# Slots chosen by transposes, unit 0 in two column parts, and an earlier third chunk of w_out

## The chip, the core and the metric

The kernel runs on one core of one Trainium2 chip. The time is the device time of one execution in microseconds (us), and the median of three runs is the measure. The chain of engines is TensorE (PE; PEld is its weight loading), VectorE (DVE), ScalarE (ACT), GpSimd (POOL), which has nothing to do here, and SyncE (SP), whose queue issues the transfers.

## What is computed

Three layers in a row. Sigmoid attention (4 batches, 12 heads, 448 tokens, 64 wide) gives x of 1792 tokens by 768. A soft mixture of 8 experts with 4 slots each (32 slots) follows, and then a last layer with a cosine gate:

```python
slot_input = d.T @ x                       # 32 slots x 768
h = np.maximum(slot_input[e] @ w1[e], 0.0) # per expert, 4 slots
slot_out[e] = h @ w2[e]
x = c @ slot_out                           # 1792 x 768
h = x @ w_in                               # 768 x 2048
g = h * np.cos(h)
out = g @ w_out                            # 2048 x 768
```

w_in and w_out come as 64-bit floats and are narrowed to 32 bits on the chip.

## The kernel before

The last layer never forms x. It first makes M = slot_out @ w_in, 32 slots by 2048 columns, and then h = c M per block. M is laid out in the tile m4 as four parts of 32 rows (twice the high part of M, twice its rest), and ct4 holds the weights c in the same four parts, so that one matmul of 128 by 128 by 448 gives h of one unit.

**The second expert layer.** The experts go in two groups g of four. w2_rows and part multiply a group's 16 wide slots (four column strips of 32) by w2 as it lands, into PSUM tiles e2[g, k] (k = 0: 512 columns, k = 1: 256). Only the diagonal blocks of these are wanted. w2_out copies e2 to SBUF (for group 1 the left half on ScalarE and the right half on VectorE). choose then makes, for each 128 columns of the model (chunk c, six of them), a product with the small 0/1 tile pick, which both turns the chunk and picks the 16 slots. twice copies the result from PSUM to s_acc with every slot doubled.

**M.** wide_m(so, c, pairs) adds chunk c's share to M's first 512 columns, in strips of 64 rows (the doubled slots): pair 0 and pair 1 are two PSUM tiles of 2 x 128 columns. rest_m does the same for the other 1536 columns, in four strips of 32 rows side by side. m_hi and m_lo write m4's parts for the first four f. m_split does it for the rest: one cast on ScalarE (mh), one difference on VectorE (ml), and 16 transfers that spread them to m4.

**Units.** A unit u = (t, f) is a block of 448 columns of tokens by 128 columns of w_in. wave(u) is its h matmul, in one of two PSUM banks (ps_h), and ScalarE's scaling; wave_end is ScalarE's rounding; frac(u) is VectorE's centring and ScalarE's sine; product(u) is VectorE's h * cos(h) and the last reader of the h bank, so the h matmul of unit u + 2 waits for product(u). out_unit(u, os) multiplies the result by the chunk f of w_out, six tiles o of 128 rows. For the first SOME = 6 units this is a full 32-bit product in two passes. From unit 6 on it is three products of rounded parts, which need wh and wl.

**w_out.** A chunk f is narrowed by wo_abs(f), one ScalarE step of 768 columns, and wo_steps(f), three VectorE steps. Then wo_hi(f) on ScalarE and wo_lo(f) on VectorE make the parts wh and wl, and wo_lo loads chunk f + 6 into the raw tile that is free.

**Order.** Every engine runs its instructions in the order in which the program gives them (manual_schedule). Up to unit 1 the order is written out by hand (lines 1012 to 1058). From then on a loop over u issues, for each unit: product(u + 1), upper, frac(u + 2), the first two output tiles of u, wave(u + 3), steps from the list later (some_of), lower, the other four tiles. The list holds wo_abs, wo_steps, wo_hi and wo_lo in order with a price each (0.55, 0.95, 0.95 for the steps, 0.95 for wo_lo, nothing for those of ScalarE). A unit brings a budget of 3.6 in the first six units and 1.9 later, and the list is worked off from its head while the budget lasts.

Of the kernel before, what the change touches and what calls it, by code (L numbers as in the profile page):

```python
# [10 lines left out]
F32 = mybir.dt.float32  # L11
# [14 lines left out]
P = 128  # L26
# [35 lines left out]
def fused(ctx: ExitStack, tc: tile.TileContext, qk, vv, phi, w1, w2, w_in, w_out, out):  # L62
# [629 lines left out]
    def wide_m(so, c, pairs=range(2)):  # L692

        for i in pairs:
            for n in range(2):
                at = (2 * i + n) * P
                nc.tensor.matmul(  # L697
                    m_ps[i][n * D:(n + 1) * D, 0:P], so.rearrange("p r s -> p (r s)"), wi[:, c, at:at + P],
                    start=c == 0, stop=c == KD - 1,
                )  # L700

    def rest_m(so, c):

        for j in range(4):
            at = MC + 3 * P * j
            nc.tensor.matmul(  # L706
                m_ps[2][j * NS:(j + 1) * NS, 0:3 * P], so[:, 0], wi[:, c, at:at + 3 * P],
# [4 lines left out]
    def so4_of(c):  # L712
        return s_acc.rearrange("p a f -> p (a f)")[:, c * 2 * NS:(c + 1) * 2 * NS].rearrange("p (r s) -> p r s", r=2)

    so2 = s_acc.rearrange("p a f -> p (a f)")[:, 512:512 + 4 * NS].rearrange("p (c r s) -> p c r s", c=2, r=2)

    with ExitStack() as ex:
# [3 lines left out]
        with tc.manual_schedule():  # L721
# [67 lines left out]
            def w2_out(g, k):  # L789

                n = 256 if k else 512
                if g == 0:
                    nc.scalar.copy(sos[g, k], e2[g, k][:, 0:n])
                    return
                nc.scalar.copy(sos[g, k][:, 0:n // 2], e2[g, k][:, 0:n // 2])
                nc.vector.tensor_copy(sos[g, k][:, n // 2:n], e2[g, k][:, n // 2:n])

            def choose(g, k):

                for c in range(2 if k else 4):  # L800
                    at = (256 if k else 0) + c * NS + 16 * g
                    nc.tensor.matmul(
                        (e2[0, 1] if k else ps_so)[:, at:at + 16], sos[g, k][:, c * P:(c + 1) * P],
                        pick[:, g], start=True, stop=True,
                    )

            def twice(out, chosen, n):

                nc.vector.tensor_copy(
                    out, chosen.rearrange("p (c s) -> p c s", c=n).unsqueeze(2).to_broadcast([P, n, 2, NS])  # L810
                )
# [11 lines left out]
            pick = exp_.tile([P, 2, NS // 2], F32, name="pick")  # L823
            for g in range(2):
                for j in range(4):
                    at = 36 * j + 16 * g
# [320 lines left out]
```

## Time and profile before

| | before |
|---|---|
| median of 3 runs | 528.34 us (528.27 to 529.23) |
| the profiled execution | 528.16 us, span of the core 526.5 us |
| PE busy | 507.0 us (96% of the span) |
| DVE busy | 302.7 us (57%) |
| ACT busy | 301.3 us (57%) |
| DMA | 98.91 MB, 188 GB/s on the mean |
| mean granted TensorE clock | 0.999 |

The attention and the first expert matmuls take the first 215 us. From 215 to 258 us TensorE waits for w2 as it lands. The stretch that the change edits lies between 239 and some 285 us. From there to the end TensorE runs the units. Times in the rows are us from the span's start. A busy PE is not PE at its peak, since matmuls are pipelined and their ends are modelled: the start of the next one tells how long one holds the engine. A full 32-bit matmul stands as two records (passes).

### The profile page before, as it was taken

The numbers are of one execution on the slowest core, as the hardware profiler recorded it, in microseconds if no ns is written. First come the engines' busy times: TensorE is split into PE (matmuls) and PEld (weight loads), VectorE is DVE, ScalarE is ACT, GpSimd is POOL, SyncE is SP. The second block draws the span as 40 slices with busy tenths as digits, with TensorE's granted clock in tenths as the row PEclk, the third lists the DMA queues.
The fourth block names the chain that finished last, engine by engine and source line by source line (L and its number), as shares of the span: only waits on it lengthen the run. The fifth ranks groups of instructions, "written<-read, shape, count | busy, mean of one in ns | idle before, by whom it ended". The sixth has DMA issues, their size and how long they took to land.

```text
span 526.5 us, 8037 instructions
## 1 busy us (share of the span) xinstructions
PE 507.0 (96%) x3134; PEld 321.9 (61%) x3134; DVE 302.7 (57%) x591; ACT 301.3 (57%) x488; POOL 2.1 (0%) x16
## 2 busy tenths in 40 slices
PE   8999999999999997968999999999999999999997
PEld 4333333334334532314544599999999999999996
DVE  4545895685683324300179897999664464564442
ACT  5877768668667310200158687887665555555551
POOL 1000000000000000000000000000000000000000
PEclk9999999999999999999999999999999999999999
DMA  6798899787447899999954331330020020020002
GB/s 227 240 338 309 296 332 359 255 333 270 151 150 247 264 407 415 414 415 413 390 210 110 120 120 61 120 121 2 0 106 0 2 105 1 9 98 0 1 0 105
DMA packets 30117, 98.91 MB, mean 188 GB/s; under 512 B 3200, under 2 KB 11264, under 8 KB 30080
## 3 DMA queue, kind: packets, MB, share of 16 engines
q1 hardware_dynamic: 30080, 98.42, 51.9%
q8 instruction: 24, 0.39, 0.3%
q14 instruction: 13, 0.11, 0.1%
HBM read 92.11 MB, written 5.51 MB: 185 GB/s over the span
## 4 chain that ended last, share of the span: by engine, by line
PE 83%; DMA 11%; DVE 3%; ACT 1%; issue 1%; SPq 0%
PE o L994 43%; PE av L315 14%; DMA w<-in_w 11%; PE sc L295 11%; PE h L945 3%; PE xn L335 2%; PE idle L371 1%; PE lg L362 1%; PE h L734 1%; PE so L773 1%; PE sl L502 1%; PE m L706 1%; DVE wi L1006 1%; PE lt L386 1%; PE m L697 1%
## 5 line engine op out<-in xcount | busy, mean ns | idle before, releaser
L994 PE MATMUL o<-gh,wl 128*128 128x448 f32 x348 | 126.4, 363 | 0.0
L994 PE MATMUL o<-gl,wh 128*128 128x448 f32 x348 | 126.3, 363 | 0.0
L994 PE MATMUL o<-gh,wh 128*128 128x448 f32 x348 | 125.9, 362 | 0.0
L304 ACT ACTIVATE a<-sc,bias_s 128x896 f32<-128x896 f32 x72 | 70.3, 1006 | 31.7 <-PE sc L295 31.6
L994 PEld LDWEIGHTS o<-gh,wl 128*128 128x128 f32 x348 | 65.5, 188 | 5.4 <-issue 0.2
L994 PEld LDWEIGHTS o<-gh,wh 128*128 128x128 f32 x348 | 65.2, 187 | 4.8 <-issue 0.2
L994 PEld LDWEIGHTS o<-gl,wh 128*128 128x128 f32 x348 | 65.3, 188 | 3.5
L315 PE MATMUL av<-a,v 128*64 128x448 f32 x288 | 64.7, 556 | 0.0
L974 ACT CAST gh<-wi 128x448 fp32r<-128x448 f32 x58 | 32.8, 566 | 51.5 <-PE o L994 44.5
L960 DVE SCALAR_TENSOR_TENSOR wi<-wi 128x448 f32<-128x448 f32 x63 | 39.2, 622 | 35.1 <-ACT wi L953 35.1
L979 DVE TENSOR_TENSOR gl<-wi,gh 128x448 fp32r<-128x448 f32 x58 | 36.2, 624 | 33.0 <-ACT gh L974 32.6
L947 ACT ACTIVATE wi<-h 128x448 f32<-128x448 f32 x63 | 34.1, 542 | 26.7 <-PE h L945 26.1
L295 PEld LDWEIGHTS <-hi 64*128 64x128 f16 x384 | 19.4, 95 | 37.6 <-issue 20.2
L968 DVE TENSOR_TENSOR wi<-h,wi 128x448 f32<-128x448 f32 x63 | 38.9, 617 | 0.9 <-ACT wi L963 0.9
L773 PE MATMUL so<-w,zone 128*32 128x256 f32 (+1 forms) x256 | 31.5, 490 | 7.8 <-DMA w<-in_w 7.8
L963 ACT ACTIVATE wi<-wi 128x448 f32<-128x448 f32 x63 | 36.2, 575 | 2.6 <-DVE wi L960 2.6
L953 ACT ACTIVATE wi<-wi 128x448 f32<-128x448 f32 x63 | 36.4, 578 | 2.0
L295 PE MATMUL sc<-hi 64*128 64x448 f16 x192 | 35.2, 359 | 0.4 <-ACT a L304 0.4
L315 PEld LDWEIGHTS av<-a,v 128*64 128x64 f32 x288 | 16.4, 135 | 29.9 <-issue 29.2
L295 PE MATMUL sc<-hi,lo 64*128 64x448 f16 x192 | 34.4, 354 | 0.3
L295 PE MATMUL sc<-lo,hi 64*128 64x448 f16 x192 | 34.3, 354 | 0.0
L273 DVE CAST hi<-raw 128x896 f16<-128x896 f32 x23 | 14.3, 624 | 34.3 <-DMA raw<-in_qk 34.2
(175 smaller groups left out, 573.2 us busy)
## 6 DMA issues: line engine op xcount, KB each, us to landing
w<-in_w SPq DMA_DIRECT2D x28, 768.0 KB, 15.1
w<-in_w SPq DMA_DIRECT2D x30, 512.0 KB, 6.4
wi<-in_w_in SPq DMA_DIRECT2D x24, 512.0 KB, 6.9
wo<-in_w_out SPq DMA_DIRECT2D x16, 768.0 KB, 4.5
w<-in_w SPq DMA_DIRECT2D x11, 1024.0 KB, 7.1
raw<-in_qk SPq DMA_DIRECT2D x23, 448.0 KB, 3.9
v<-in_vv SPq DMA_DIRECT2D x24, 224.0 KB, 4.3
out_t<-wi SPq DMA_DIRECT2D x24, 224.0 KB, 2.0
```

Source lines behind the costliest of these rows:

```text
L295: nc.tensor.matmul(ps[:, j, 0:S], keys[at, first:first + P], q[at, 0:S], start=n == 0, stop=n == len(terms) - 1)
L304: nc.scalar.activation(a[at], ps[at], AF.Sigmoid, bias=bias_s[at[0]], scale=qk_scale)
L315: nc.tensor.matmul(av[i][js, 0:S], v32[i][:, vc:vc + D], a[:, j], start=g == 0, stop=g == 3)
L773: nc.tensor.matmul(e2[g, k][j * NS:(j + 1) * NS, 0:n], h1[g][:, c, j * NS:(j + 1) * NS], w(j), start=c == 0, stop=c == F // P - 1,)
L947: nc.scalar.activation(ph, h, AF.Copy, bias=0.25, scale=inv2pi)
L953: nc.scalar.activation(tn, ph, AF.Copy, bias=magic)
L960: nc.vector.scalar_tensor_tensor(out=ph, in0=tn, scalar=-magic, in1=ph, op0=ALU.add, op1=ALU.subtract)
L963: nc.scalar.activation(tn, ph, AF.Sin, scale=-2.0 * math.pi)
L968: nc.vector.tensor_mul(g, hs.pop(u), tn)
L974: nc.scalar.copy(gs[u][1], gs[u][0])
L979: nc.vector.tensor_sub(gs[u][2], gs[u][0], gs[u][1].bitcast(F32))
L994: nc.tensor.matmul(ps, w[:, cols], g, start=begins and n == 0, stop=ends and n == len(terms) - 1)
```

## The change

The change edits five things.

- choose turns each chunk with a transpose instead of a product with pick, and a new keep_slots copies the wanted columns with one strided VectorE copy, once and not doubled. pick and twice are gone. w2_out of group 1 is one ScalarE copy. The slots of chunks 0 to 3 lie in l_all, of 4 and 5 in s_acc (slots_of).
- wide_m has four strips of 32 rows instead of two of 64.
- Unit 0's scaling, rounding, centring, sine, product and outputs are done in two halves of 224 columns (first, second).
- m_split is cut in two (m_split_hi, m_split_lo), and the hand-written order is a new one. In it chunk 2 of w_out is narrowed whole ahead of unit 2 (wo_abs(2) behind unit 1's sine, wo_steps(2, 3) behind unit 1's product), and wo_abs(3) stands ahead of wave(3). The list later no longer has these steps.
- wave(4) stands behind all of unit 1's outputs and behind what the list issues there. The warming matmuls of one of three steps are gone.

```diff
--- before.py
+++ after.py
@@ -692,11 +692,11 @@
     def wide_m(so, c, pairs=range(2)):
 
         for i in pairs:
-            for n in range(2):
-                at = (2 * i + n) * P
+            for k in range(4):
+                at = (2 * i + k // 2) * P
                 nc.tensor.matmul(
-                    m_ps[i][n * D:(n + 1) * D, 0:P], so.rearrange("p r s -> p (r s)"), wi[:, c, at:at + P],
-                    start=c == 0, stop=c == KD - 1,
+                    m_ps[i][k * NS:(k + 1) * NS, 0:P], so, wi[:, c, at:at + P], start=c == 0,
+                    stop=c == KD - 1,
                 )
 
     def rest_m(so, c):
@@ -704,15 +704,16 @@
         for j in range(4):
             at = MC + 3 * P * j
             nc.tensor.matmul(
-                m_ps[2][j * NS:(j + 1) * NS, 0:3 * P], so[:, 0], wi[:, c, at:at + 3 * P],
+                m_ps[2][j * NS:(j + 1) * NS, 0:3 * P], so, wi[:, c, at:at + 3 * P],
                 start=c == 0, stop=c == KD - 1,
             )
 
 
-    def so4_of(c):
-        return s_acc.rearrange("p a f -> p (a f)")[:, c * 2 * NS:(c + 1) * 2 * NS].rearrange("p (r s) -> p r s", r=2)
-
-    so2 = s_acc.rearrange("p a f -> p (a f)")[:, 512:512 + 4 * NS].rearrange("p (c r s) -> p c r s", c=2, r=2)
+    def slots_of(c):
+
+        if c < 4:
+            return l_all.rearrange("p b c s -> p (b c s)")[:, 256 + c * NS:256 + (c + 1) * NS]
+        return s_acc.rearrange("p a f -> p (a f)")[:, 512 + (c - 4) * NS:512 + (c - 3) * NS]
 
     with ExitStack() as ex:
         zone = ex.enter_context(reuse("zone", bufs=1)).tile([P, 2 * F], F32, name="zone")
...
-                n = 256 if k else 512
-                if g == 0:
-                    nc.scalar.copy(sos[g, k], e2[g, k][:, 0:n])
-                    return
-                nc.scalar.copy(sos[g, k][:, 0:n // 2], e2[g, k][:, 0:n // 2])
-                nc.vector.tensor_copy(sos[g, k][:, n // 2:n], e2[g, k][:, n // 2:n])
+                nc.scalar.copy(sos[g, k], e2[g, k][:, 0:256 if k else 512])
 
             def choose(g, k):
 
+                ps = (e2[0, 1][:, 256:] if k else ps_so).rearrange("p (c m) -> p c m", m=P)
                 for c in range(2 if k else 4):
-                    at = (256 if k else 0) + c * NS + 16 * g
-                    nc.tensor.matmul(
-                        (e2[0, 1] if k else ps_so)[:, at:at + 16], sos[g, k][:, c * P:(c + 1) * P],
-                        pick[:, g], start=True, stop=True,
-                    )
-
-            def twice(out, chosen, n):
-
+                    nc.tensor.transpose(ps[:, c], sos[g, k][:, c * P:(c + 1) * P], ident)
+                return ps
+
+            def keep_slots(g, k, ps):
+
+                out = (s_own[:, 512:512 + 2 * NS] if k else l_own[:, 256:]).rearrange("p (c s) -> p c s", s=NS)
+                v = ps[:, :, 16 * g:16 * g + 4]
                 nc.vector.tensor_copy(
-                    out, chosen.rearrange("p (c s) -> p c s", c=n).unsqueeze(2).to_broadcast([P, n, 2, NS])
+                    out[:, :, 16 * g:16 * g + 16].rearrange("p c (j k) -> p c j k", j=4),
+                    bass.AP(v.tensor, v.offset, [v.ap[0], v.ap[1], [36, 4], v.ap[2]]),
                 )
 
             def keep_warm(n):
...
-            pick = exp_.tile([P, 2, NS // 2], F32, name="pick")
-            for g in range(2):
-                for j in range(4):
-                    at = 36 * j + 16 * g
-                    nc.vector.tensor_copy(pick[:, g, 4 * j:4 * j + 4], ident[:, at:at + 4])
             w1_group(0)
             w1_group(1)
             nc.scalar.activation(sine, ident[:, 0:1], AF.Sin)
-            so4 = s_own[:, 0:8 * NS].rearrange("p (c r s) -> p c r s", c=4, r=2)
...
             for c in range(0, F // P - 2, 2):
                 w2_rows(1, c)
                 if c == 0:
-                    choose(0, 0)
-                    choose(0, 1)
-                keep_warm(4)
+                    ps = [choose(0, k) for k in range(2)]
+                    for k in range(2):
+                        keep_slots(0, k, ps[k])
+                if c < F // P - 4:
+                    keep_warm(4)
...
-            choose(1, 0)
+            ps = choose(1, 0)
             part(1, 1, F // P - 2, lambda j: w[:, 0, j], 256)
+            keep_slots(1, 0, ps)
+            m_ps.update({k: bank((4, 3, 5)[k], f"m{k}") for k in range(3)})
+            for c in range(2):
+                wide_m(slots_of(c), c, [0])
             part(1, 1, F // P - 1, lambda j: w[:, 1, j], 256)
-            twice(so4, ps_so[:, 0:4 * NS], 4)
             w2_out(1, 1)
-            m_ps.update({k: bank((4, 3, 5)[k], f"m{k}") for k in range(3)})
-            for c in range(4):
-                wide_m(so4[:, c], c, [0])
-            choose(1, 1)
-            twice(so2, e2[0, 1][:, 256:256 + 2 * NS], 2)
-            for c in range(2):
-                wide_m(so4[:, c], c, [1])
+            for c in range(2, 4):
+                wide_m(slots_of(c), c, [0])
+            keep_slots(1, 1, choose(1, 1))
+            wide_m(slots_of(0), 0, [1])
 
 
     wctx.close()
@@ -911,17 +904,25 @@
         src, hi, lo = m_parts(f)
         nc.vector.tensor_sub(lo, src, hi.bitcast(F32))
 
-    def m_split():
-
-        mh, ml = [ring[:, (12 + k) * S:(12 + k) * S + 3 * P] for k in range(2)]
-        nc.scalar.copy(mh.bitcast(F32R), m_ps[2][:, 0:3 * P])
-        nc.vector.tensor_sub(ml.bitcast(F32R), m_ps[2][:, 0:3 * P], mh)
-        for j in range(4):
+    mh, ml = [ring[:, (12 + k) * S:(12 + k) * S + 3 * P] for k in range(2)]
+
+    def spread(js, groups):
+
+        for j in js:
             cols = slice(MC + 3 * P * j, MC + 3 * P * (j + 1))
-            for g in range(4):
+            for g in groups:
                 nc.sync.dma_start(
                     out=m4[g * NS:(g + 1) * NS, cols].bitcast(F32), in_=(mh, ml)[g // 2][j * NS:(j + 1) * NS]
                 )
+
+    def m_split_hi():
+        nc.scalar.copy(mh.bitcast(F32R), m_ps[2][:, 0:3 * P])
+        spread([0], (0, 1))
+
+    def m_split_lo():
+        nc.vector.tensor_sub(ml.bitcast(F32R), m_ps[2][:, 0:3 * P], mh)
+        spread([0], (2, 3))
+        spread(range(1, 4), range(4))
 
     SOME = 6
     units = [(t, f) for t in range(2) for f in range(SOME)] + [(2, f) for f in range(NF)]
@@ -936,7 +937,28 @@
 
     hs, tmp = {}, {}
 
-    def wave(u, rounded=True):
+    first, second, whole_s = slice(0, S // 2), slice(S // 2, S), slice(0, S)
+
+    def scaled(u, cols):
+        nc.scalar.activation(tmp[u][0][:, cols], hs[u][:, cols], AF.Copy, bias=0.25, scale=inv2pi)
+
+    def rounded(u, cols):
+        nc.scalar.activation(tmp[u][1][:, cols], tmp[u][0][:, cols], AF.Copy, bias=magic)
+
+    def centred(u, cols):
+        ph, tn, g = tmp[u]
+        nc.vector.scalar_tensor_tensor(
+            out=ph[:, cols], in0=tn[:, cols], scalar=-magic, in1=ph[:, cols], op0=ALU.add, op1=ALU.subtract
+        )
+
+    def sined(u, cols):
+        nc.scalar.activation(tmp[u][1][:, cols], tmp[u][0][:, cols], AF.Sin, scale=-2.0 * math.pi)
+
+    def times(u, cols):
+        ph, tn, g = tmp[u]
+        nc.vector.tensor_mul(g[:, cols], hs[u][:, cols], tn[:, cols])
+
+    def wave(u, both=True):
         if u >= len(units):
             return
         t, f = units[u]
@@ -944,29 +966,20 @@
         h = hs[u] = ps[:, 0:S]
         nc.tensor.matmul(h, m4[:, f * P:(f + 1) * P], ct4[:, t * S:(t + 1) * S], start=True, stop=True)
         ph, tn, g = tmp[u] = [spare[k] if u == 0 else buf(3 * (u % 4) + k) for k in range(3)]
-        nc.scalar.activation(ph, h, AF.Copy, bias=0.25, scale=inv2pi)
-        if rounded:
-            wave_end(u)
-
-    def wave_end(u):
-        ph, tn, g = tmp[u]
-        nc.scalar.activation(tn, ph, AF.Copy, bias=magic)
+        scaled(u, whole_s if u else first)
+        if u and both:
+            rounded(u, whole_s)
 
     def frac(u):
 
-        if u >= len(units):
-            return
-        ph, tn, g = tmp[u]
-        nc.vector.scalar_tensor_tensor(
-            out=ph, in0=tn, scalar=-magic, in1=ph, op0=ALU.add, op1=ALU.subtract
-        )
-        nc.scalar.activation(tn, ph, AF.Sin, scale=-2.0 * math.pi)
+        if u < len(units):
+            centred(u, whole_s)
+            sined(u, whole_s)
 
     def product(u):
         if u < len(units):
-            ph, tn, g = tmp.pop(u)
-            nc.vector.tensor_mul(g, hs.pop(u), tn)
-            gs[u] = [g]
+            times(u, whole_s)
+            gs[u] = [tmp.pop(u)[2]]
 
     def upper(u):
         if SOME <= u < len(units):
...
+    def out_half(cols, os):
+
+        for o in os:
+            if cols == first:
+                acc[o] = bank(o, f"o0_{o}")
+            nc.tensor.matmul(
+                acc[o][:, cols], whole(0)[:, o * P:(o + 1) * P], gs[0][0][:, cols],
+                start=cols == first, stop=False,
+            )
 
     def out_unit(u, os):
         t, f = units[u]
@@ -1011,51 +1034,62 @@
     with tc.manual_schedule():
         for f in range(A_SLOTS, WO_SLOTS):
             load_wo(f)
-        both = [so4_of(c) for c in range(4)] + [so2[:, c] for c in range(2)]
+        both = [slots_of(c) for c in range(KD)]
         wo_abs(0, 2)
         wide_m(both[4], 4, [0])
         wide_m(both[5], 5, [0])
-        wo_steps(0)
         m_hi(0, nc.vector.tensor_copy)
         m_lo(0)
         m_hi(1)
+        wide_m(both[1], 1, [1])
         wide_m(both[2], 2, [1])
-        wide_m(both[3], 3, [1])
         wave(0)
+        wo_steps(0, 2)
+        m_lo(1)
+        for c in range(3, KD):
+            wide_m(both[c], c, [1])
+        rounded(0, first)
+        centred(0, first)
+        scaled(0, second)
+        sined(0, first)
+        rounded(0, second)
         wo_steps(0)
-        m_lo(1)
-        wo_steps(0, 2)
-        wide_m(both[4], 4, [1])
-        wide_m(both[5], 5, [1])
-        for c in range(2):
-            rest_m(both[c], c)
-        wave(1, False)
-        frac(0)
-        wave_end(1)
-        wo_steps(0)
-        for c in range(2, 4):
-            rest_m(both[c], c)
-        wo_abs(1)
-        product(0)
-        wo_steps(0)
+        times(0, first)
+        centred(0, second)
+        rest_m(both[0], 0)
+        rest_m(both[1], 1)
         m_hi(2)
         m_hi(3)
-        frac(1)
+        wave(1, False)
+        sined(0, second)
+        rounded(1, whole_s)
+        wo_abs(1)
+        wo_steps(0)
         m_lo(2)
         m_lo(3)
-        out_unit(0, range(3))
-        for c in range(4, KD):
+        times(0, second)
+        gs[0] = [tmp.pop(0)[2]]
+        out_half(first, range(3))
+        rest_m(both[2], 2)
+        out_half(second, range(3))
+        wo_steps(0, 2)
+        frac(1)
+        wo_abs(2)
+        for c in range(3, KD):
             rest_m(both[c], c)
+        m_split_hi()
+        wo_steps(1, 3)
+        m_split_lo()
         product(1)
-        wo_steps(1, 2)
-        m_split()
-        wo_abs(2)
-        out_unit(0, range(3, 5))
+        for cols in (first, second):
+            out_half(cols, range(3, 5))
         wave(2)
+        for cols in (first, second):
+            out_half(cols, range(5, NO))
+        wo_abs(3)
         wave(3)
-        wo_steps(1)
+        wo_steps(2, 3)
         frac(2)
-        out_unit(0, range(5, NO))
 
 
 
@@ -1068,9 +1102,9 @@
             return f if f < SOME else 2 * SOME + f
 
         for f in range(2, NF + 2):
-            if f + 1 < NF:
+            if 2 < f < NF - 1:
                 add(0, 99, lambda f=f: wo_abs(f + 1))
-            for time in (.55, .95, .95) if f < NF else ():
+            for time in (.55, .95, .95) if 2 < f < NF else ():
                 add(time, first(f), lambda f=f: wo_steps(f))
             if f == 2:
                 add(0, 99, lambda: wo_hi(0))
@@ -1098,7 +1132,8 @@
             if ends:
                 time -= 1.9
             out_unit(u, range(2))
-            wave(u + 3)
+            if u > 1:
+                wave(u + 3)
             if u + 1 >= SOME:
                 time = some_of(time - .95, 0) + .95
             else:
@@ -1106,6 +1141,8 @@
             lower(u + 1)
             time = min(some_of(time, u + 1), .95)
             out_unit(u, range(2, NO))
+            if u == 1:
+                wave(4)
 
 
 # ---- launch: one core ----
```

## Rows read from the trace of the kernel before

**Rows 1.** The chain of waits before unit 4: start, length, what ran.

```profile
277.09 0.47 ACT wi L963
...
277.59 0.64 DVE wi L968
```

**Rows 2.** Busy time by stretch: length, PE, PEld, DVE, ACT, POOL; granted clock, DMA.

```profile
225.00:230.00 5.00, 3.01 (x19) 0.72 (x23) 0.00 (x0) 0.00 (x0) 0.00 (x0) 1.00 1.01 408
...
280.00:285.00 5.00, 5.00 (x15) 2.74 (x14) 4.83 (x8) 5.00 (x8) 0.00 (x0) 1.00 0.32 75
```

**Rows 3.** TensorE in order of time: start, length, line, tiles, count, idle before.

```profile
254.53 1.16 PE L818 MATMUL warm<-ident 128*128 128x128 f32 x8
...
258.93 1.08 PE L802 MATMUL ps_so<-pick,s_acc 128*128 128x16 f32 x8
259.94 1.07 PE L773 MATMUL so<-w,zone 128*32 128x256 f32 x16
...
262.51 1.55 PE L697 MATMUL m<-wi,s_acc 128*64 128x128 f32 x24
264.33 0.47 PE L945 MATMUL h<-ct,m 128*128 128x448 f32 x1 [0.27 <-DVE m L912]
264.73 0.66 PE L697 MATMUL m<-wi,s_acc 128*64 128x128 f32 x8
...
269.02 2.50 PE L994 MATMUL o<-wo,wo 128*128 128x448 f32 x6 [0.38 <-issue]
...
275.65 1.67 PE L994 MATMUL o<-wi,wo 128*128 128x448 f32 x4
278.27 0.47 PE L945 MATMUL h<-ct,m 128*128 128x448 f32 x1 [0.95 <-DVE wi L968]
278.57 4.67 PE L994 MATMUL o<-wi,wo 128*128 128x448 f32 x12
282.73 0.71 PE L945 MATMUL h<-ct,m 128*128 128x448 f32 x1
...
287.44 0.71 PE L945 MATMUL h<-ct,m 128*128 128x448 f32 x1
```

**Rows 4.** TensorE in order of time, transposes ahead of the second expert matmul.

```profile
213.50 0.66 PE L756 MATMUL h1p<-ident,zone 128*128 128x128 f32 x4
```

**Rows 5.** ScalarE in order of time, copies of slots and steps of units.

```profile
231.46 0.86 ACT L793 COPY s_acc<-so 128x512 f32<-128x512 f32 x2 [16.79 <-PE so L773]
258.50 0.37 ACT L795 COPY s_acc<-so 128x256 f32<-128x256 f32 x1 [26.19 <-PE so L773]
...
264.84 0.54 ACT L947 ACTIVATE wo<-h 128x448 f32<-128x448 f32 x1 [0.23 <-PE h L945]
265.41 0.58 ACT L953 ACTIVATE wo<-wo 128x448 f32<-128x448 f32 x1
...
281.17 2.55 ACT L893 CAST wh<-wo 128x768 fp32r<-128x768 f32 x3
```

**Rows 6.** VectorE in order of time, pick's copies, then slots and chunks.

```profile
185.83 0.66 DVE L827 COPY pick<-ident 128x4 f32<-128x4 f32 x8
...
258.91 0.42 DVE L796 COPY s_acc<-so 128x256 f32<-128x256 f32 x1 [42.92 <-ACT s_acc L795]
...
278.66 0.55 DVE L179 TENSOR_SCALAR wf<-wf 128x768 uint32<-128x768 uint32 x1
279.25 0.96 DVE L180 SCALAR_TENSOR_TENSOR wf<-wo,wf 128x768 uint32<-128x768 uint32 x1
280.24 0.96 DVE L183 SCALAR_TENSOR_TENSOR wo<-wo,wf 128x768 uint32<-128x768 uint32 x1
...
281.78 0.62 DVE L968 TENSOR_TENSOR wi<-h,wi 128x448 f32<-128x448 f32 x1
...
284.71 0.95 DVE L896 TENSOR_TENSOR wl<-wo,wh 128x768 fp32r<-128x768 f32 x1
```

**Rows 7.** SP's queue, the spreading transfers of M.

```profile
273.52 10.13 SPq L922 DMA_DIRECT2D m<-wi  x16
```

## The prediction

> **What bounds the kernel now.** I began with the busy shares by stretch [rows 2], went to the chain of waits at the place of the change [rows 1], and then read the three engines' queues there in order of time [rows 3 to 6]. TensorE is the bound from the first output matmul on: from 278.57 one unit of the last layer follows the next with no gap, 4.71 us each (the next units' h matmuls stand at 282.73 and 287.44, [rows 3]), and it stays so but for a few tenths at the ends of the groups. A shift of TensorE at unit 4 is therefore a shift of the end. Ahead of that there are holes: 0.27 us before unit 0's h matmul, 0.38 before its first output, and 0.95 before unit 4's h matmul at 278.27 [rows 3]. The last one is the chain's [rows 1]: unit 4's h needs the PSUM bank of unit 2, and that is free only when ScalarE's sine (277.09) and VectorE's product (277.59) of unit 2 are done. The other thing to see is that past this point VectorE and ScalarE are full too, 4.83 and 5.00 us of 5.00 in 280 to 285 [rows 2]. TensorE has no idle time there, but its two helpers have none either.
>
> **How I price a queue.** Each engine works in program order. From the rows: a ScalarE step of 768 columns keeps its engine 0.80 to 0.82 (three in 2.55, the last one 0.91 long, [rows 5]), one of 448 columns 0.45, or 0.58 when the next needs its result. The three VectorE steps of a narrowed chunk take 0.59, 0.99 and 0.87 (starts at 278.66, 279.25, 280.24), a residue of w_out 0.87, a product or a centring 0.54 of the queue and 0.62 to its end [rows 6]. A hand-over costs 0.03 to 0.06. Twelve output passes in 4.67 make 0.375 a pass. Walked with these lengths, the rows of before come out within 0.1 us up to unit 6, so I walk the changed program in the same way.
>
> **The change, part by part.**
>
> *The slots, up to unit 1.* Choosing by products costs 0.92 for a group of four chunks and half of that for two: 1.38 [rows 3]. Four transposes stand at 0.12 apart (four in 0.66 with the last one's tail, [rows 4]): 0.72 for six, so -0.66. They wait for one ScalarE copy of 512 columns, 0.59 (the pair in 0.86 less the second's share, [rows 5]), from 258.50 to 259.09; before, the first product began at 258.93 behind half a copy: +0.22. VectorE's strided copy of 64 values is not in the trace; its bounds are 0.16 (one of the eight 4-column copies: 0.66 less seven steps of 0.07) and 0.42 (the 256-column copy, [rows 6]); I take 0.30, the middle, as its 64 values lie between. With it, TensorE waits 0.05 for the first chunk's slots, 0.10 for the second ScalarE copy and 0.18 for the last two chunks' slots: +0.33. The first layer's products for the four narrow parts are now four of 32 columns where there were two of 64. Not in the trace at 128 columns; the nearest rows are sixteen records of 256 columns in four strips in 1.07 and twenty-four of 64-wide strips in 1.55 [rows 3], which both say that strips run side by side: 0.22 a chunk, as before. The other bound is strip after strip, 0.44 a chunk, or +2.0 for what lies ahead of unit 1. As those products now have the same shape as their neighbours, about four mode changes of 0.1 fall away (unit 0's h matmul holds TensorE from 264.33 to 264.73 with narrow products behind it, where one among outputs adds 0.20 to the twelve passes of 4.51, [rows 3]): -0.41. Unit 0 in halves: a half costs more than half, 0.35 on ScalarE and 0.39 on VectorE (between the 256- and 448-column rows, [rows 5, 6]), but its first half is ready at 266.3 where the outputs of before had to wait until 269.0, so that hole goes, 0.38 and the 0.08 by which the first pass was longer: -0.45. The sum is -0.97: unit 1's first output moves from 275.65 to about 274.6. The eight small copies for the pick tile, early on, and the four warming matmuls [rows 3] lay beside loads: nothing.
>
> [...]
>
> *The third chunk, and the held matmul.* ScalarE's first step for it now comes at 275.0, VectorE's three stand at 273.4 to 276.0, behind unit 1's product, in time that was idle (VectorE's product of unit 2 waits another 1.0 for the sine). The sine of unit 2 ends at 277.4 and its product at 278.1, much as before (278.2): what the earlier start brings is eaten by 0.80 of ScalarE work that now stands ahead of it. But TensorE does not stand still meanwhile: with unit 4's h behind unit 1's outputs, these run from 274.6 to 279.1, the h matmul follows at once, and unit 2 begins at 279.3 instead of 281.57 (278.57 and eight passes): a lead of 2.24. The sixteen spreading transfers [rows 7] start a little earlier and the four that unit 4 needs have landed by 277: nothing waits.
>
> *What is late next.* With the third chunk out of the list, the list of spare steps stands one chunk further on. Unit 1's budget of 3.6 now buys ScalarE wo_hi(0), (1), (2), wo_abs(4), wo_hi(3), wo_abs(5), and VectorE the three steps of chunk 3 and wo_lo(0). Two things are queued behind these. On VectorE the product of unit 3: centring of unit 3 to 278.54, then 2.45 and 0.87, so the product ends at 282.48 and frees unit 5's bank. TensorE is there at 280.8 and waits 1.75: of the lead 0.49 is left. On ScalarE it is worse, since unit 4's two steps are now behind the list instead of ahead of it: the sine of unit 3 at 278.69 to 279.17, six times 0.80 to 283.97, then 0.58 and 0.58 to 285.13. VectorE's centring of unit 4 stands at the head of its queue from 282.4 and waits 2.77 for that; behind it are chunk 4's three steps (2.45), wo_lo(1) (0.87) and the product of unit 4, 289.01 to 289.63, which frees the bank that unit 6's h needs. TensorE is there at 287.24: 2.45 of waiting. Lead 0.49 less 2.45 is 1.96 late, and 0.17 more at unit 7's h: 2.13 late. From there on TensorE is the bound again, nothing gives it back, and the holes at the ends of the groups are the same.
>
> So the profiled execution would go from 528.16 to 530.3; the median shown lies 0.18 above it, and 528.34 + 2.13 is 530.5.
>
> **The rivals.** (a) *The lead is kept, faster.* If the product of unit 4 is there when TensorE asks at 287.2, and that of unit 3 at 280.8, the 2.24 stay: 526.1. The place is the six ScalarE steps and VectorE's five steps behind unit 3's centring; it decides from the point where the six take 0.4 each instead of 0.80. For it speaks that VectorE has one chunk less to do later; against it that three in a row took 2.55 [rows 5]. 0.08. (b) *Lead and wait about cancel.* At 0.60 for a ScalarE step the wait at unit 6 is 1.2 shorter and the end 0.73 late: 529.1. The same happens if the head gains 1.4 more than I sum. 0.13. (c) *The four strips run one after the other*: 12 chunk products of 0.22 more ahead of unit 1, some of it hidden: 2.0 on top, 532.5. Rows of both widths speak against it [rows 3]. 0.05. (d) *The column parts do not take effect*, since a consumer of one half waits for both: unit 0's first outputs then stand at 268.1 and all behind them moves 1.6: 532.1. Against it: the first outputs of before began at 269.02 while VectorE still wrote the chunk's other columns. 0.03. (e) *The clock falls* where the four warming matmuls stood. [...] 0.02. [...]
>
> **How the numbers follow.** The forecast, ScalarE's list ahead of unit 4, has 0.69: 530.5, and between 529.3 and 531.7 with its unknowns (transposes at 0.24, a strided copy at 0.16 or 0.5, halves at 0.30 or 0.45, mode changes at nothing). A run here tells 0.2% from no change, 1.06 us: faster is under 527.3, slower over 529.4. Slower is the forecast with (c), (d), (e): 0.79; same is (b): 0.13; faster is (a): 0.08. The range reaches over (b), (c) and (d): 528.8 to 532.6; outside are (a), (e) and tails.
>
> **What would show it.** Right: transposes from about 259.15; unit 1's outputs from 274.6 with no hole inside; unit 2 at about 279.3; then two waits of TensorE for VectorE's product at the h matmuls of units 5 and 6, of 1.7 and 2.4; six ScalarE steps of 768 columns in a row between unit 3's sine and unit 4's first step; VectorE idle 2.8 before unit 4's centring. Wrong: no hole at unit 6's h, or a ScalarE order in which unit 4's steps come before the list, or strips that take 0.44 a chunk. The forecast falls as a whole if ScalarE gets through the list by 281.

## The result and the profile after

| | before | after |
|---|---|---|
| median | 528.31 us (20 executions) | 532.48 us (20 executions) |
| ratio, 95% interval | | 1.0064 [1.0046, 1.0082] |
| the profiled execution | 528.16 us, span 526.5 | 532.38 us, span 530.3 |
| mean granted TensorE clock | 0.999 | 0.993 |

The change makes the kernel slower, by 4.2 us between the medians and 3.4 us by the ratio. One of the twenty executions of the changed kernel took 993.23 us: the median counts it, the ratio does not, and without it the median is 532.38. A second set of executions of the same pair gave 1.0056 [1.0036, 1.0076], which is 3.0 us.

Not all of this lies in the span, the time from the core's first instruction to its last. What the table has outside it grows by 0.4 us, from 1.7 (528.16 less 526.5) to 2.1 (532.38 less 530.3). It is so in every execution whose span was taken: 1.63 to 1.77 for the kernel before, 2.08 to 2.20 for the changed one. No trace here shows what it consists of.

The loads of w2 end up to 3 us apart from one execution to another (the zero points of the fourteen traces below lie between 256.38 and 259.54), and everything behind them moves with that. So I count each h matmul from the start of the last eight expert matmuls of 512 columns in its own trace, the zero point, and subtract the same in the trace of before. In the following, "unit 6 stands 2.38 late" means this. The zero point of before, TensorE in order of time (start, length, line, tiles, count, idle before):

```profile
257.32 1.06 PE L773 MATMUL so<-w,zone 128*32 128x512 f32 x8
```

TensorE after the change, in order of time, from its zero point on:

```profile
257.42 1.06 PE L774 MATMUL so<-w,zone 128*32 128x512 f32 x8 [1.02 <-DMA w<-in_w]
...
260.29 0.62 PE L697 MATMUL m<-wi,l_all 128*32 128x128 f32 x16
...
263.92 0.47 PE L967 MATMUL h<-ct,m 128*128 128x448 f32 x1 [0.29 <-DVE m L905]
...
266.71 1.29 PE L999 MATMUL o<-wo,wo 128*128 128x224 f32 x6
...
274.92 4.67 PE L1017 MATMUL o<-wi,wo 128*128 128x448 f32 x12
279.08 0.72 PE L967 MATMUL h<-ct,m 128*128 128x448 f32 x1
279.64 1.67 PE L1017 MATMUL o<-wi,wo 128*128 128x448 f32 x4
282.75 0.48 PE L967 MATMUL h<-ct,m 128*128 128x448 f32 x1 [1.44 <-DVE wi L959]
283.07 4.67 PE L1017 MATMUL o<-wi,wo 128*128 128x448 f32 x12
289.92 0.47 PE L967 MATMUL h<-ct,m 128*128 128x448 f32 x1 [2.18 <-DVE wi L959]
290.23 6.37 PE L1017 MATMUL o<-wi,wo 128*128 128x448 f32 x12
296.09 0.72 PE L967 MATMUL h<-ct,m 128*128 128x448 f32 x1
```

The 0.38 ahead of unit 0's outputs and the 0.95 at unit 4's h [rows 3] are gone: unit 1's twelve passes run without a hole and unit 4's h follows at 279.08. In their place stand two longer holes, 1.44 at unit 5's h and 2.18 at unit 6's, both ended by VectorE's product (L959). And the twelve passes behind the second one take 6.37 where every other group of twelve takes 4.67. The h matmuls say the same: unit 4's is 0.71 late (it was moved behind the outputs), unit 5's 0.08 early (282.75 - 257.42 against 282.73 - 257.32), unit 6's 2.38 late, unit 7's 3.84 late (one unit of 4.71 behind 287.44 in before [rows 3]), and so it stays to the end, 3.8.

ScalarE, where unit 4's two steps (L943, L946) stand now behind the list, and VectorE, which waits for them at its centring (L950):

```profile
278.93 0.58 ACT L955 ACTIVATE wi<-wi 128x448 f32<-128x448 f32 x1 [1.28 <-DVE wi L950]
279.41 2.50 ACT L886 CAST wh<-wo 128x768 fp32r<-128x768 f32 x3
281.81 0.90 ACT L176 ACTIVATE wf<-wo 128x768 f32<-128x768 f32 x1
282.61 0.88 ACT L886 CAST wh<-wo 128x768 fp32r<-128x768 f32 x1
283.39 0.92 ACT L176 ACTIVATE wf<-wo 128x768 f32<-128x768 f32 x1
284.19 0.54 ACT L943 ACTIVATE wi<-h 128x448 f32<-128x448 f32 x1
284.77 0.58 ACT L946 ACTIVATE wi<-wi 128x448 f32<-128x448 f32 x1
```

```profile
282.08 0.62 DVE L959 TENSOR_TENSOR wi<-h,wi 128x448 f32<-128x448 f32 x1
285.38 0.62 DVE L950 SCALAR_TENSOR_TENSOR wi<-wi 128x448 f32<-128x448 f32 x1 [2.68 <-ACT wi L946]
...
289.25 0.62 DVE L959 TENSOR_TENSOR wi<-h,wi 128x448 f32<-128x448 f32 x1
```

Six steps of 768 columns in 4.78 (279.41 to 284.19), then unit 4's, then VectorE's centring after a wait of 2.68, then four steps of VectorE, and at 289.25 the product for which TensorE waits at unit 6's h.

The last piece is in the windows (length; PE, PEld, DVE, ACT, POOL; granted clock, DMA share, GB/s):

```profile
285.00:290.00 5.00, 2.82 (x9) 1.20 (x7) 4.55 (x7) 3.44 (x6) 0.00 (x0) 1.00 0.42 158
290.00:291.00 1.00, 1.00 (x3) 0.62 (x4) 0.96 (x3) 0.77 (x3) 0.00 (x0) 0.94 0.41 98
291.00:294.00 3.00, 3.00 (x5) 1.35 (x4) 2.96 (x4) 1.93 (x4) 0.00 (x0) 0.50 0.57 229
```

From 291 to 294 the granted clock is 0.50, in a stretch in which TensorE is never idle. It fell about 1 us behind the end of the second hole. So the 3.8 are two parts: the two holes less the lead, 2.3, and the low clock, 1.5 (a trace of the same kernel without the fall, below, gives the 2.3). The second part was not in my sum, nor was the 0.4 outside the span.

### The profile page after: what moved, and what is told of

The parts are those of the page before. It is cut to its first block, busy times and chain, and to the rows that moved or that the text cites. A ratio compares the mean times of both kernels' runs of the same rounds, so it can differ in the third digit from the quotient of the medians.

```text
span 530.3 us, 8114 instructions
## 1 busy us (share of the span) xinstructions
PE 507.5 (96%) x3174; PEld 322.1 (61%) x3174; DVE 302.4 (57%) x585; ACT 302.7 (57%) x491; POOL 2.1 (0%) x16
## 4 chain that ended last, share of the span: by engine, by line
PE 73%; DMA 16%; DVE 7%; ACT 2%; issue 1%; SPq 0%; DVEq 0%; ACTq 0%
PE o L1017 41%; DMA w<-in_w 12%; PE av L315 11%; PE sc L295 8%; DMA raw<-in_qk 4%; PE h L967 3%; PE xn L335 2%; PE h L735 2%; DVE lo L276 2%; PE lg L362 1%; DVE hi L273 1%; PE sl L502 1%; PE o L999 1%; PE m L706 1%; PE idle L371 1%
## 5 line engine op out<-in xcount | busy, mean ns | idle before, releaser
L950 DVE SCALAR_TENSOR_TENSOR wi<-wi 128x448 f32<-128x448 f32 x63 | 39.2, 622 | 37.5 <-ACT wi L946 37.5
L943 ACT ACTIVATE wi<-h 128x448 f32<-128x448 f32 x63 | 34.2, 543 | 28.4 <-PE h L967 27.9
L774 PE MATMUL so<-w,zone 128*32 128x512 f32 (+1 forms) x256 | 31.8, 490 | 8.5 <-DMA w<-in_w 8.5
L959 DVE TENSOR_TENSOR wi<-h,wi 128x448 f32<-128x448 f32 x63 | 38.9, 618 | 0.8 <-ACT wi L955 0.8
L946 ACT ACTIVATE wi<-wi 128x448 f32<-128x448 f32 x63 | 36.4, 578 | 2.0
```

The lines of the kernel that those rows point to most:

```text
L774: nc.tensor.matmul(e2[g, k][j * NS:(j + 1) * NS, 0:n], h1[g][:, c, j * NS:(j + 1) * NS], w(j), start=c == 0, stop=c == F // P - 1,)
L943: nc.scalar.activation(tmp[u][0][:, cols], hs[u][:, cols], AF.Copy, bias=0.25, scale=inv2pi)
L946: nc.scalar.activation(tmp[u][1][:, cols], tmp[u][0][:, cols], AF.Copy, bias=magic)
L950: nc.vector.scalar_tensor_tensor(out=ph[:, cols], in0=tn[:, cols], scalar=-magic, in1=ph[:, cols], op0=ALU.add, op1=ALU.subtract)
L959: nc.vector.tensor_mul(g[:, cols], hs[u][:, cols], tn[:, cols])
```

## The experiments

Two theories stand against each other for the holes: that of the forecast (unit 4's two ScalarE steps, and VectorE's product of unit 3, stand behind a list that is too long there), and that it is the place of unit 4's h matmul by itself, whatever the list holds. For the 1.5, that idle time brought the low clock, or that it fell by chance. All ratios are to the kernel before, on the same chip. In the diffs "-" is the changed kernel unless another is named.

**Unit 4's wave ahead of the list.**

```diff
-            if u > 1:
-                wave(u + 3)
+            if u == 1:
+                out_unit(u, range(2, NO))
+            wave(u + 3)
...
-            out_unit(u, range(2, NO))
-            if u == 1:
-                wave(4)
+            if u > 1:
+                out_unit(u, range(2, NO))
```

> The changed kernel with unit 4's h matmul and its two ScalarE steps still behind all of unit 1's outputs, but ahead of what the list issues there. Theory A (ScalarE's list ahead of unit 4's steps makes the hole at unit 6): the hole of 2.2 us ahead of unit 6's h is gone, the one ahead of unit 5's h stays and grows to some 2.4 us, since the list still stands ahead of unit 3's product on VectorE; TensorE from unit 6 on about 0.4 us later than in the kernel before, 528.8 us, and up to 1.5 us more where the clock falls behind that one hole. Rival B (VectorE has too much to do there in any order, so a wait is only moved): a hole of 1.5 us or more stays at unit 6's h, and the time stays at 530 us or above.

Median 530.63, ratio 1.0035 [1.0013, 1.0057], profiled 528.79. TensorE:

```profile
283.05 0.48 PE L967 MATMUL h<-ct,m 128*128 128x448 f32 x1 [2.04 <-DVE wi L959]
```

The hole at unit 6's h is gone (its row has no idle time any more); the one at unit 5's remains. The units from 8 on stand 0.55 late (about 0.4 expected; the hole that stays is 2.04 where some 2.4 were expected). So 1.75 of the 2.30 were ScalarE's list ahead of unit 4's steps. There was one hole of 2.04 and the clock stayed at 1.00 from 280 to 300.

**The same with a short list.** As above, and

```diff
-            time += 3.6 if u + 1 < SOME else 1.9
+            time += 0.6 if u == 1 else 3.6 if u + 1 < SOME else 1.9
```

> As x1, and unit 1's budget for the list is 0.6 us instead of 3.6 us, so that VectorE's product of unit 3 is no longer behind a chunk and a residue. Theory A: no hole at the h matmuls of units 4, 5 and 6, the lead of about 2 us with which unit 2 begins is kept to the end, 526.1 us. Rival B: VectorE's steps that are put off come due at unit 3 or 4 and TensorE waits for them there; 527.5 us or above.

Median 527.04, ratio 0.9965 [0.9947, 0.9983], profiled 525.98: faster than both kernels. TensorE:

```profile
278.42 0.72 PE L967 MATMUL h<-ct,m 128*128 128x448 f32 x1
...
280.13 0.72 PE L967 MATMUL h<-ct,m 128*128 128x448 f32 x1
```

No hole at the h of units 4, 5 and 6, and all units from 5 on are 2.03 to 2.05 early (unit 5's: 280.13 - 256.75 against 282.73 - 257.32; about 2 expected). This is the lead that the change had made and lost: rival (a) of the prediction, with the list out of the way.

**The short list alone.** Only the budget above; unit 4's wave stays behind the list.

> The changed kernel with one change: unit 1's budget is 0.6 instead of 3.6, and wave(4) stays behind all of unit 1's outputs and behind what the list issues. It tells the length of the list from the place of wave(4). Theory (ScalarE's list ahead of unit 4's two steps is the cause, by its length): the same walk gives no hole at unit 5's h, one of 2.1 before unit 3's outputs (their chunk is narrowed later), one of 0.4 at unit 6's h, and units from 6 on 0.27 later than before: median 0.3 above that of the kernel before, and 1.9 under that of the change where the clock stays (3.3 where it fell). Rival (the place of wave(4) behind the outputs is what costs, whatever stands in the list): the hole of 2.2 at unit 6's h stays, and the median is within 0.5 of the change.

Median 528.77, ratio 0.9996 [0.9978, 1.0015]. TensorE:

```profile
286.76 1.78 PE L1017 MATMUL o<-wi,wo 128*128 128x448 f32 x4 [1.77 <-DVE wo L183]
```

The holes at the h of units 5 and 6 become one of 1.77 (2.1 expected), now before unit 3's outputs, for the last narrowing step of their chunk. That step stands on VectorE behind the centring of unit 4, which still waits for ScalarE. The units from 8 on are 0.39 late (0.27 by the walk). The rival, that the place alone costs, would have kept the hole of 2.2: it falls. The short list is worth 1.9 here, and the place of the wave the other 2.4 (0.39 to -2.04).

**The place alone, in the kernel before.** The diff of the first experiment against the kernel before, with a budget of 2.5 at unit 1.

> The kernel before with the place of one step changed: wave(4) stands behind all of unit 1's outputs and ahead of the list, whose budget at unit 1 is 2.5; no transposes, no column parts, no earlier third chunk. It tells whether the earlier narrowing of the third chunk is needed for the lead of 2.0 that the short list kept. Theory (it is): the hole of 0.95 at unit 4's h goes, but TensorE then waits about 1.05 before unit 2's outputs for VectorE's last step of the third chunk; the same walk gives units from 2 to about 28 0.2 earlier and the end between 0.2 earlier and 0.2 later, median within 0.3 of before. Rival (the place of unit 4's h alone brings it): no hole before unit 2's outputs and everything from unit 2 on 0.95 earlier, median 0.9 under before.

Median 528.41, ratio 0.9997 [0.9976, 1.0018]. TensorE:

```profile
281.08 0.71 PE L945 MATMUL h<-ct,m 128*128 128x448 f32 x1
282.52 1.78 PE L994 MATMUL o<-wi,wo 128*128 128x448 f32 x4 [0.73 <-DVE wo L183]
```

Unit 4's h no longer waits, but unit 2's outputs do, for VectorE's last step of chunk 2 (0.73, where 1.05 were expected). Units from 5 on are 0.2 early, those of the last half 0.08. So the third chunk has to be narrowed earlier, as the change does, for the lead to exist at all.

**The slots alone, in the kernel before.** Transposes, one strided copy and four strips; unit 0 whole and the old order.

```diff
-                    m_ps[i][n * D:(n + 1) * D, 0:P], so.rearrange("p r s -> p (r s)"), wi[:, c, at:at + P],
+                    m_ps[i][k * NS:(k + 1) * NS, 0:P], so, wi[:, c, at:at + P], start=c == 0,
...
-                    nc.tensor.matmul(
+                    nc.tensor.transpose(ps[:, c], sos[g, k][:, c * P:(c + 1) * P], ident)
```

> The kernel before with only the first part of the change: slots by transposes, one strided copy, four strips of 32 columns, one warming step fewer; order from unit 0 on as before. Theory: TensorE's unit 0 begins 0.4 us earlier and nothing takes that back, 527.9 us. Rival (strips one after the other, or waits in the chain of copies): unit 0 begins at the same time or later, 528.3 us or above. The clock in the stretch before the last expert matmul stays at 1.00.

Median 528.28, ratio 0.9983 [0.9966, 1.0000]. TensorE:

```profile
267.92 2.50 PE L987 MATMUL o<-wo,wo 128*128 128x448 f32 x6 [0.38 <-issue]
...
277.16 0.48 PE L938 MATMUL h<-ct,m 128*128 128x448 f32 x1 [0.95 <-DVE wi L961]
```

All units are 0.44 early; the two holes of before are there, unchanged (0.38 and 0.95). The slots bring 0.44 and nothing gives it back.

**Unit 0's outputs whole.**

```diff
-        out_half(first, range(3))
         rest_m(both[2], 2)
-        out_half(second, range(3))
+        out_unit(0, range(3))
...
-        for cols in (first, second):
-            out_half(cols, range(3, 5))
+        out_unit(0, range(3, 5))
         wave(2)
-        for cols in (first, second):
-            out_half(cols, range(5, NO))
+        out_unit(0, range(5, NO))
```

> The changed kernel with unit 0's outputs in whole passes again behind both column parts (scaling, rounding, sine and product stay in two parts, the third narrow product of M's rest moves ahead of the outputs). It measures by itself what the first half's outputs bring. The walk behind the forecast gives: unit 0's outputs begin when the second half's product is done, unit 1's first output 0.73 later than with halves, and as the two later holes are the same the end is 0.73 later too: median 0.7 above that of the change. Rival: the hole ahead of unit 0's outputs only moves, since TensorE has narrow products to do meanwhile; then unit 1's first output is within 0.2 and the median the same.

Median 531.37, ratio 1.0050 [1.0026, 1.0074], profiled 530.57. TensorE:

```profile
267.31 2.50 PE L1017 MATMUL o<-wo,wo 128*128 128x448 f32 x6 [0.60 <-issue]
...
282.45 0.47 PE L967 MATMUL h<-ct,m 128*128 128x448 f32 x1 [1.47 <-DVE wi L959]
...
289.61 0.47 PE L967 MATMUL h<-ct,m 128*128 128x448 f32 x1 [2.18 <-DVE wi L959]
289.92 4.67 PE L1017 MATMUL o<-wi,wo 128*128 128x448 f32 x12
```

A hole of 0.60 stands ahead of unit 0's outputs, and all units are 0.60 later than with halves (unit 4's 1.32 late against 0.71; units from 8 on 2.90 against the 2.30 of two holes without a low clock). The expected 0.73 was a little large. The medians don't show it (531.37 against 532.48 and 531.77 of the changed kernel), but their intervals are about 1 us wide to each side. This kernel's trace has the same two holes and no low clock: the twelve passes at 289.92 take 4.67. So the fall doesn't follow the holes every time.

**Is the low clock the holes'?** First the holes filled: matmuls of 64 columns that nobody reads, into unused columns of a PSUM bank, six ahead of unit 5's h and nine ahead of unit 6's.

```diff
             out_unit(u, range(2))
+            for _ in range({2: 6, 3: 9}.get(u, 0)):
+                nc.tensor.matmul(acc[1][:, S:512], ident, ident[:, 0:64], start=False, stop=False)
```

> The changed kernel with matmuls that nobody reads ahead of the h matmuls of unit 5 (six) and unit 6 (nine), into PSUM columns that are not in use. They take the place of most of the two waits. [...] Rival D (the clock falls for another reason, or the fall costs nothing): the clock is at 0.50 behind unit 6's h as in the changed kernel, or the time stays at its 532 us.

Median 532.06, ratio 1.0049 [1.0029, 1.0069]. TensorE, and then the windows:

```profile
284.29 0.47 PE L967 MATMUL h<-ct,m 128*128 128x448 f32 x1 [0.15 <-DVE wi L959]
...
291.50 0.47 PE L967 MATMUL h<-ct,m 128*128 128x448 f32 x1 [0.27 <-DVE wi L959]
```

```profile
290.00:295.00 5.00, 4.73 (x21) 3.15 (x21) 4.93 (x8) 3.84 (x6) 0.00 (x0) 1.00 0.43 157
```

The clock stays at 1.00 and the units from 8 on are 2.3 late: the queues' price alone. Of rival D's two signs the clock of 0.50 is absent, and the time of 532 is there: the traced execution took 532.51, since its loads ended 1.5 later (zero point 258.96), and the median, 532.06, is not clearly below those of the changed kernel. A second trace of it, with the second trace of the changed kernel and a third one:

> The changed kernel with 6 and 9 matmuls that nobody reads in the holes ahead of the h matmuls of units 5 and 6, unchanged from the earlier run, one more look. If it is the idle time of the holes that lowers the clock, it stays at 1.00 from 275 to 300 and the h matmuls from unit 7 on stand 2.3 later than before; if the clock falls here too, for 3.4 us, they stand 3.7 later and idle time is not what decides.

> The changed kernel unchanged, to see whether the low clock behind the second hole belongs to it. If it does, the granted clock is 0.50 again from some 0.5 us after the second hole (behind unit 6's h matmul) for about 3.5 us, the h matmuls from unit 7 on stand 3.8 later than before, counted from the last expert matmuls of 512 columns, and the median is again about 532.5. If the fall was chance, the clock stays at 1.00 in 285 to 300, the h matmuls from unit 7 on stand 2.1 to 2.4 later (the two holes alone), and the median of some executions with and some without it is 531 to 532.

> The changed kernel unchanged, one more look at the granted clock behind the hole at unit 6's h. With the fall (0.50 for about 3.5 us) the h matmuls from unit 7 on stand 3.8 later than before, without it 2.1 to 2.4.

The filled kernel again has 1.00 in every window from 258 to 300 and 2.3 late. The changed kernel's second trace (531.47) has holes of 1.44 and 2.20, then

```profile
290.00:291.00 1.00, 1.00 (x3) 0.52 (x2) 0.96 (x2) 0.97 (x2) 0.00 (x0) 0.50 1.06 399
...
291.00:294.00 3.00, 3.00 (x7) 1.41 (x6) 3.00 (x5) 1.85 (x3) 0.00 (x0) 0.62 0.34 98
```

and its units from 7 on are 3.85 late. Its third trace (532.56) has the same holes and no fall:

```profile
291.58 0.47 PE L967 MATMUL h<-ct,m 128*128 128x448 f32 x1 [2.20 <-DVE wi L959]
291.88 4.67 PE L1017 MATMUL o<-wi,wo 128*128 128x448 f32 x12
```

```profile
291.00:294.00 3.00, 2.42 (x7) 1.48 (x8) 2.93 (x5) 2.44 (x5) 0.00 (x0) 1.00 0.60 213
```

Its units from 8 on are 2.30 late (unit 8's h at 300.91 - 259.06 against 296.87 - 257.32; its time is as long because its loads ended 1.6 later).

Two filled traces without a fall are few where the unfilled holes had it in two of four. The mean clock was taken in every execution. In the fourteen traces it is 0.993 only in the two that have this fall and also the earlier low stretch named in the last section; all others have 0.995 or more. It was 0.993 or less in 14 of 32 executions of the changed kernel, in none of 11 of the filled one, and in 7 of 85 of the kernel before. That speaks for the holes.

Then the opposite: the faster order with one long hole made on purpose, by six ScalarE steps that make a part of w_out again.

```diff
                 out_unit(u, range(2, NO))
+                for _ in range(6):
+                    wo_hi(0)
             wave(u + 3)
```

> The faster order of an earlier run (wave(4) ahead of the list, unit 1's budget 0.6) with six ScalarE steps added ahead of unit 4's scaling; each makes again, with the same result, the rounded part of chunk 0, so it is pure waiting. By the walk VectorE waits for unit 4's centring, and with it the chunk of unit 3 comes late: one hole in TensorE of 3.7 before unit 3's outputs and one of 0.4 at unit 6's h, units from 7 on 1.9 later than before. It tells whether a single long hole lowers the clock as the two of the change did. If the sum of idle time counts, the granted clock falls to 0.50 behind the hole and the units from 7 on are 3.0 to 3.5 later; if it was something else in the changed kernel, the clock stays at 1.00 and they are 1.9 later.

Its execution took 534.59. TensorE, and the windows:

```profile
290.64 3.35 PE L1017 MATMUL o<-wi,wo 128*128 128x448 f32 x4 [3.99 <-DVE wo L183]
```

```profile
290.00:291.00 1.00, 0.36 (x1) 0.36 (x2) 1.00 (x2) 1.00 (x2) 0.00 (x0) 0.82 0.00 0
...
292.00:294.00 2.00, 2.00 (x4) 0.87 (x3) 1.65 (x3) 1.97 (x4) 0.00 (x0) 0.50 0.69 169
```

The clock falls to 0.50 behind the one hole of 3.99, in a kernel that has none of the two of the change; four passes take 3.35, where the kernel with the short list alone had 1.78, and the units from 8 on are 3.9 late. That is 2.0 more than the walk without a fall (0.3 of it since the hole is 3.99 and not 3.7), and more than the 3.0 to 3.5 that I expected with one. In all fourteen traces the clock between 215 and 520 us is under 1.00 in three places only, and each is behind these long holes. So idle time of TensorE is what the runs point to, and not the changed kernel's other parts; the one long hole was traced once. What decides that two holes of 1.44 and 2.2 brought it in two of four traces stays open.

**One more product in the first hole.** On the faster order:

```diff
         wide_m(both[2], 2, [1])
+        wide_m(both[3], 3, [1])
         wave(0)
...
-        for c in range(3, KD):
+        for c in range(4, KD):
```

> The faster order (wave(4) ahead of the list, unit 1's budget 0.6) with one narrow product of M (chunk 3, second pair) moved ahead of unit 0's h matmul, into the hole of 0.29 in which TensorE waits there for VectorE. The walk: the hole falls to under 0.1 and all behind unit 1 stands 0.1 to 0.2 earlier, so that the h matmuls from unit 5 on are 2.1 to 2.25 earlier than before (2.04 without it); median 0.1 to 0.2 under the one without it, which the spread cannot tell. Rival: unit 0's h is held up by the product and unit 0's two parts come later; then the h matmuls from unit 5 on are 1.8 to 2.0 earlier.

Median 526.73, ratio 0.9962 [0.9944, 0.9979]; the units from 5 on are 2.03 early, with or without it. The hole of 0.29 at unit 0's h is gone and unit 1's h came 0.2 earlier, but the first outputs wait all the same for VectorE's product of the first half (266.11 and 0.39 long):

```profile
266.56 1.41 PE L999 MATMUL o<-wo,wo 128*128 128x224 f32 x6
```

Both expectations missed: neither a gain nor a loss.

## Why the prediction was right, and what it lacked

The sign was right, and so was the mechanism: the two waits, the six ScalarE steps in a row and VectorE's wait of 2.7 stand where they were forecast. The time lies in the range of 528.8 to 532.6, though at its upper end and above the forecast's own 529.3 to 531.7. That it lies inside is in part luck: the range reached so high for rivals (c) and (d), and neither happened (strips side by side; unit 0's first outputs at 266.71, not 268.1). Two other things, which the sum did not have, filled that room. The steps, by the h matmuls:

- *The head, -0.97 at unit 1's first output*: 274.92 - 257.42 against 275.65 - 257.32, -0.83. The slots alone gave -0.44 where their four terms sum to -0.52 (no run shows the term of the mode changes, -0.41, by itself), so unit 0 in halves is left with -0.39 where I had -0.45. VectorE's strided copy takes 0.23 and 0.19, nearer to the lower bound than the 0.30 that I took. The strips run side by side: sixteen records of 128 columns in 0.62, which rival (c) denied.
- *Unit 2, a lead of 2.24*: 2.03. Unit 4's h follows unit 1's outputs with no hole.
- *The wait at unit 5's h, 1.75*: 1.95 by the h matmuls (2.03 early to 0.08 early). The row's idle time is shorter, 1.44, as it counts from a modelled end.
- *The wait at unit 6's h, 2.45*: 2.46. Behind the six ScalarE steps unit 4's begins at 284.19 (283.97 forecast), VectorE waits 2.68 (2.77). Moving the wave ahead of the list took this hole away, and shortening the list as well took both.
- *+0.17 at unit 7*: the third trace has unit 7's h at 2.55 late, 0.15 more than unit 6's, but unit 8's at 2.30. The sum of the queues is 2.30 where I had 2.13.
- *The median*: 528.34 + 2.13 left out the clock, which falls behind the second hole in some executions, for 1.5 us, and the 0.4 outside the span. The ratios of the changed kernel, 3.0 and 3.4 us, lie between the two holes alone (2.3 and 0.4) and these with the fall (3.8 and 0.4).
- *Rival (b)* had a slip: with a wait 1.2 shorter, 2.13 late becomes 0.93, not 0.73.

The main term that failed is one that is not there, the clock. I asked of every engine what is late next, but of the clock only in rival (e), where the warming matmuls had been; there it stayed at 1.00 in every trace. Its chance of 0.02, and its place outside the range, were my estimate, and no run shows a fall there or its price. In the kernel before, the stretch of 225 to 230 is busy 3.01 of 5.00 at a clock of 1.00 [rows 2]. After the change, the stretch of 285 to 290 is busy 2.82 of 5.00, nearly the same share, and the clock fell behind it. The difference that the traces show is how the idle time lies, in one piece of 2.18 after the change, and in pieces of 0.85 between loads there; TensorE of the kernel before in order of time:

```profile
225.29 1.04 PE L773 MATMUL so<-w,zone 128*32 128x512 f32 x2 [0.84 <-DMA w<-in_w]
227.19 1.05 PE L773 MATMUL so<-w,zone 128*32 128x512 f32 x2 [0.85 <-DMA w<-in_w]
229.08 2.34 PE L773 MATMUL so<-w,zone 128*32 128x512 f32 x24 [0.85 <-DMA w<-in_w]
```

Whether it is the piece or the sum that counts, no run tells apart. The clock stood at 0.50 behind the hole of 3.99 and, in two of four traces, behind the two holes, and I should have asked for the clock at the holes that my own walk gave.

## What to carry to other kernels

Walk every engine's queue in program order with durations from the trace, and go on past the wait that is removed: what was moved ahead stands in front of something, here a list of spare steps that slid by one chunk and held up the next two units. An early step pays only if the list behind it is shortened with it (2.3 late against 2.0 early, with one step moved and one budget changed). The low clock of 0.50 behind TensorE's long idle pieces was a term of its own here, 1.5 us behind the two holes, in two of four traces and absent in the others.

## What the runs showed of the hardware

- The granted clock fell to 0.50 for some 3 us behind a hole of 3.99 (one trace), and in two of four traces behind holes of 1.44 and 2.2 that lie 7 us apart; behind single holes of 0.73, 1.77 and 2.04 (one trace each) it stayed at 1.00, as it did in both traces with the holes filled by unread matmuls of 64 columns. It cost 1.5 us behind the two holes, against a trace without the fall, and an estimated 1.7 behind the one, against the walk, on work that was never idle.
- The clock also stood at 0.93 on the mean from 200 to 225, ahead of the changed part, in nine of the fourteen traces, the kernel before with the slots alone among them, and at 1.00 in the others. One execution's mean clock therefore doesn't tell whether the later fall was there; only the windows do.
- Outside the span the kernel before has 1.7 us and the changed kernel 2.1; with the slots alone it is 1.8, and every kernel made from the changed one has 2.1 to 2.2, whatever its order. Why is open.
